# A fused attention and FFN kernel: FFN2 of batches 2 to 7 for pairs of token tiles by seven products instead of eight

## The chip, the core and the metric

The kernel runs on one core of a Trainium2 chip. The metric is the device time of one execution in microseconds (us); the number given for a kernel is the median of several runs. The core has five engines that work side by side, each through its own queue of instructions in order: TensorE (PE, matrix products; its weight loads are listed as PEld), VectorE (DVE), ScalarE (ACT), GpSimd (POOL) and SyncE (SP). Here POOL issues the loads from the main memory and SP the stores and the transposes by DMA. PE writes its sums to PSUM, eight banks of 128 x 512 numbers in f32; DVE and ACT read them from there and write to SBUF.

## The reference

```python
scores = scale * np.matmul(q, k.transpose(0, 1, 3, 2))      # 8 batches, 12 heads, 448 tokens, 64 columns; scale = 1/8
attn = np.maximum(scores, 0.0) ** 2 / S                       # S = 448
x = np.matmul(attn, v)                                        # then 3584 tokens x 768
h = x @ w_in                                                  # 768 -> 2048 (FFN1)
g = np.maximum(h, 0.0) + alpha * np.minimum(h, 0.0)
out = g @ w_out                                               # 2048 -> 768 (FFN2), in f32
```

## The kernel before

Heads are taken four at a time, so a batch has NG = 3 groups n, and there are 24 in all. A group's keys are cut into seven chunks j.

- `turn_pe` and `turn_dma` bring q and k of a group into a layout with the head's 64 columns on the partitions (tile T). From group 5 on this is `turn_dma`: DVE copies q and k into a tile `perm` (L170, two copies), and SP issues a transpose by DMA into T (L172).
- `score_mm` computes one chunk of scores: four small matmuls on PE into a pair of PSUM banks (L184). `relu` takes the pair to SBUF as `rl` on ACT ("A", L193) or DVE ("D", L195); `square` makes `at` of it, nearly always on DVE (L203).
- `attnv` multiplies the seven squared chunks of a group with v (28 matmuls, L213) into one more pair of banks; ACT empties one bank and DVE the other into xT (L223, L224).
- `f1` computes 128 of the 2048 inner columns for a batch: six matmuls (L247), then `neg` on ACT (L255) and gT on DVE (L256). A batch has 16 such units. gT holds two batches, a superblock sb, in a single buffer.
- `f2` computes one token tile of 128 for one of two column parts (256 or 512 of 768): 16 matmuls, whose fixed operand is gT and whose moving operand is w_out (L272), a copy from PSUM by ACT (L274) and two stores by SP (L280). A superblock has seven tiles; tile 3 lies half in each batch.

The kernel is written with a manual schedule: every engine's instructions stand in the order in which the program names them. PSUM banks are dealt out while the program is written, the longest unused first (`take_bank` for one, `take_pair` for a pair of neighbours); `hold` keeps a bank out of this.

From batch 2 on the order is this. The 16 f1 units of batch b come first. Chunks of the next batch's groups are computed in between: three after f1 unit 5 and three after unit 11 (`run(some(3))`), with relus on ACT, DVE, ACT. `prepare` calls `turn_dma` for a later group and sends POOL's loads of the group after next; it stands ahead of units 1 and 9 and in the FFN2 stage. Then comes the FFN2 stage with three `burst` calls between the f2 units: three chunks, the attnv of group n, two chunks, and then the squares of all five. Even batches take tiles 0 to 2 of the superblock, odd ones tiles 3 to 6. Batch 7 has no bursts.

Batches 0 and 1 have an order written out by hand. In batch 1, `turn_dma(6)` stands ahead of the f1 units' outputs, `turn_dma(7)` and `turn_dma(8)` after units 1 and 10. POOL waits for the landing of the transposes of groups 5, 6 and 8 (a copy of one element, `landed`) before it sends more loads; after group 6 these are three parts of w_out and four loads of q, k and v.

Tiles come from pools with a fixed number of buffers. A tile that takes a buffer anew waits until the last reader of the old tile has finished; for `perm` this reader is the DMA transpose.

Of the kernel before, what the change touches and what calls it, by code (L numbers as in the profile page):

```python
# [16 lines left out]
NJ = 7  # L17
# [3 lines left out]
def kernel(  # L21
# [36 lines left out]
    ident = singles.tile([128, 128], BF16)  # L58
    w_in_sb = singles.tile([128, NG, 2, d_ff], BF16)
    w_out_sb = [singles.tile([128, KF, hi - lo], BF16, name=f"w_out{i}") for i, (lo, hi) in enumerate(COLS)]  # L60
    alpha_sb = singles.tile([128, KF], F32)
# [58 lines left out]
    def load_w_out(h, lo=0, hi=KF, step=4):  # L120
        for lo in range(lo, hi, step):
            nc.gpsimd.dma_start(out=w_out_sb[h][:, lo:lo + step], in_=w_out_v[:, lo:lo + step, COLS[h][0]:COLS[h][1]])

# [12 lines left out]
    for lo, hi, eng in ((0, 4, nc.sync), (4, NJ, nc.scalar)):  # L136
        t = singles.tile([128, 2, (hi - lo) * D], F32, name=f"qfirst{lo}")
# [60 lines left out]
    def square(n, j, rl, eng="D"):  # L198
        a = at_pool.tile([128, 2, S], BF16, tag="at", name="at")
        if eng == "A":  # L200
            nc.scalar.activation(a, rl, ACTF.Square)
        else:
            nc.vector.tensor_tensor(a, rl, rl, ALU.mult)  # L203
        att[(n, j)] = a
# [38 lines left out]
    gT = {}  # L243
# [16 lines left out]
    def f1(b, ff):  # L260
        ps = take_bank()[:, :S]
        f1_mm(ps, b, ff, range(KM))
        f1_out(ps, b, ff)

    def f2(sb, c, h, parts=None):

        first_col, width = COLS[h][0], COLS[h][1] - COLS[h][0]
        o = o_pool.tile([128, d_model - CUT], F32, tag="o", name="osb")
        for lo, hi in parts or ((0, width),):
            ps = take_bank()[:, :hi - lo]  # L270
            for ff in range(KF):
                nc.tensor.matmul(ps, gT[sb][:, ff, bass.ts(c, 128)], w_out_sb[h][:, ff, lo:hi],  # L272
                                 start=(ff == 0), stop=(ff == KF - 1))
            nc.scalar.copy(o[:, lo:hi], ps)  # L274
            for u in range(2):
                blk = 2 * c + u
                b, j = 2 * sb + blk // NJ, blk % NJ
                rows = out[b * S:(b + 1) * S].rearrange("(pp j) d -> j pp d", j=NJ)
                eng = nc.scalar if u and parts else nc.sync
                eng.dma_start(out=rows[j][:, first_col + lo:first_col + hi], in_=o[64 * u:64 * u + 64, lo:hi])  # L280

# [167 lines left out]

    def some(k):  # L450
        lo = at_c[0]
        at_c[0] = min(lo + k, len(chunks))
        return [(n, j, e) for (n, j), e in zip(chunks[lo:at_c[0]], "ADA")]

    def burst(n):

        sc(some(3))
        attnv(n)
        sc(some(2))
        sq()  # L460
# [49 lines left out]
    burst(8)  # L510
    f2(0, 6, 1)

    for b in range(2, B):
# [15 lines left out]
        for i, u in enumerate(units):  # L529
            if i in at and not last:  # L530
                g = at[i]
                if g == 1:
                    prepare(n0 + 4)
                burst(n0 + g)
            if last and i == len(units) - 1:
                f2(*u, parts=((0, 384), (384, 512)))
            else:
                f2(*u)

# [29 lines left out]
```

## Time and profile before

| what | value |
|---|---|
| time, median of 3 runs | 386.65 us (385.65 to 386.66) |
| span of the profiled execution | 384.0 us |
| PE busy | 374.1 us, 97% |
| PEld busy | 205.3 us |
| DVE busy | 266.2 us, 69% |
| ACT busy | 207.6 us, 54% |
| POOL busy | 68.9 us, 18% |
| FFN1 matmuls (L247) | 768, 149.8 us |
| FFN2 matmuls (L272) | 149.8 us |
| stage of FFN2, batch 2 | 137.5 to 160.6 us |
| stage of FFN2, batch 3 | 180.4 to 208.7 us |

The profile shows one execution by its span, from the first to the last instruction; of this execution's own time beyond the span nothing is given. The runs' median is 2.65 us above the span. In the rows, the first number is busy time, and the idle time of an engine before an instruction stands with what ended it. A busy PE is not the same as a PE at its peak, since matmuls overlap in the pipeline; the chain of waits lays the pieces end to end, and its lengths per matmul are the better price.

### The profile page before, as it was taken

How to read it: one execution, taken by the hardware profiler on the slowest of the kernel's cores; microseconds unless marked ns; L12 is line 12 of the kernel's file. 1: busy time of each engine (PE TensorE's matmuls, PEld its weight loads, DVE VectorE, ACT ScalarE, POOL GpSimd, SP SyncE). 2: the span in 40 equal slices, each digit the busy share in tenths (PEclk: the TensorE clock that was granted, in tenths of full speed). 3: DMA queues.
4: the chain of work that ended last, by engine and by line, in shares of the span. 5: the costliest groups of instructions: out<-in, count | busy, mean ns of one | idle time of the engine just before them, and what ended most of it. 6: DMA issues, size and time to landing. Idle time of an engine off the chain costs nothing.

```text
span 384.0 us, 7838 instructions
## 1 busy us (share of the span) xinstructions
PE 374.1 (97%) x3171; PEld 205.3 (53%) x3192; DVE 266.2 (69%) x423; ACT 207.6 (54%) x335; POOL 68.9 (18%) x105
## 2 busy tenths in 40 slices
PE   6799999999999999999999999999999999999996
PEld 5454565555544455545565455544556445645554
DVE  3987988777657988688656887779855788526300
ACT  4988687445643754455444656546544475434321
POOL 8566050506402202022200222020000000000000
PEclk9999999999999999999999999999999999999999
DMA  9999989999995667488292772946035300120023
GB/s 145 192 204 202 186 127 199 171 178 203 224 172 109 108 113 114 105 134 119 48 167 60 134 120 53 165 76 120 15 86 88 77 1 15 43 68 2 14 68 85
DMA packets 73556, 43.29 MB, mean 113 GB/s; under 512 B 40368, under 2 KB 70064, under 8 KB 73520
## 3 DMA queue, kind: packets, MB, share of 16 engines
q0 software_dynamic: 27136, 22.58, 39.8%
q1 hardware_dynamic: 45952, 19.88, 26.8%
q8 instruction: 25, 0.41, 0.5%
q10 hardware_dynamic: 432, 0.33, 0.3%
q14 instruction: 11, 0.09, 0.1%
HBM read 45.62 MB, written 11.01 MB: 147 GB/s over the span
## 4 chain that ended last, share of the span: by engine, by line
PE 95%; DVE 2%; issue 1%; POOL 0%; ACT 0%; ACTq 0%; POOLq 0%; DVEq 0%
PE psum L247 38%; PE psum L272 38%; PE psum L184 9%; PE psum L213 8%; DVE at L203 1%; PE psum L146 1%; DVE T L165 1%; PE psum L162 1%; DVE rl L195 0%; POOL kraw L131 0%; ACT osb L274 0%; ACTq L280 0%; POOL ident masks.py:199 0%; POOL ident masks.py:197 0%; POOLq masks.py:199 0%
## 5 line engine op out<-in xcount | busy, mean ns | idle before, releaser
L272 PE MATMUL psum<-w_out,gT 128*128 128x256 bf16 (+3 forms) x891 | 149.8, 322 | 1.1
L247 PE MATMUL psum<-xT,w_in_sb 128*128 128x448 bf16 x768 | 149.8, 353 | 0.0
L272 PEld LDWEIGHTS <-gT 128*128 128x128 bf16 x912 | 86.8, 98 | 64.2 <-issue 8.2
L247 PEld LDWEIGHTS <-w_in_sb 128*128 128x128 bf16 x768 | 73.7, 98 | 72.8 <-issue 5.3
L256 DVE SCALAR_TENSOR_TENSOR gT<-neg,beta_sb,psum 128x448 bf16<-128x448 f32 x128 | 83.4, 676 | 33.8 <-ACT neg L255 33.6
L255 ACT ACTIVATE neg<-psum 128x448 f32<-128x448 f32 x128 | 69.2, 546 | 60.3 <-PE psum L247 59.2
L193 ACT ACTIVATE rl<-psum 128x896 bf16<-128x896 f32 x112 | 97.7, 930 | 1.4 <-PE psum L184 1.4
L203 DVE TENSOR_TENSOR at<-rl 128x896 bf16<-128x896 bf16 x162 | 90.5, 616 | 0.0
L195 DVE TENSOR_SCALAR rl<-psum 128x896 bf16<-128x896 f32 x56 | 60.8, 1085 | 40.4 <-PE psum L184 40.3
L274 ACT COPY osb<-psum 128x256 f32<-128x256 f32 (+3 forms) x57 | 26.9, 473 | 104.7 <-PE psum L272 97.6
L184 PE MATMUL psum<-T 64*64 64x448 bf16 x672 | 45.4, 356 | 2.1 <-DVE T L165 1.1
L100 POOL DMA_DIRECT2D qraw<-in_q_dram x23 | 16.6, 722 | 136.2 <-DVE perm L170 131.7
L213 PE MATMUL psum<-at,vraw 64*64 64x448 bf16 x672 | 36.2, 350 | 0.0
L184 PEld LDWEIGHTS <-T 64*64 64x64 bf16 x672 | 16.8, 105 | 21.0 <-issue 13.6
L213 PEld LDWEIGHTS <-vraw 64*64 64x64 bf16 x672 | 21.0, 106 | 11.7 <-issue 1.5
L224 DVE TENSOR_SCALAR xT<-psum 128x448 bf16<-128x448 f32 x24 | 15.0, 624 | 14.8 <-PE psum L213 11.0
L107 POOL DMA_DIRECT2D vraw<-in_v_dram x24 | 17.5, 732 | 4.6 <-PE psum L184 1.4
L100 POOL DMA_DIRECT2D kraw<-in_k_dram x23 | 16.7, 726 | 1.9 <-issue 1.4
L223 ACT ACTIVATE xT<-psum 128x448 bf16<-128x448 f32 x24 | 13.4, 560 | 2.3 <-PE psum L213 2.3
L170 DVE COPY perm<-qraw 128x896 bf16<-128x896 bf16 x19 | 11.6, 610 | 0.0
L170 DVE COPY perm<-kraw 128x896 bf16<-128x896 bf16 x19 | 11.6, 608 | 0.0
L117 POOL DMA_DIRECT2D w_in_sb<-in_moe_w_in_dram x16 | 10.0, 634 | 5.5 <-DMA w_in_sb<-in_moe_w_in_dram 2.3
(24 smaller groups left out, 41.6 us busy)
## 6 DMA issues: line engine op xcount, KB each, us to landing
out_dram<-osb SPq DMA_DIRECT2D x54, 128.0 KB, 2.4
vraw<-in_v_dram POOLq DMA_DIRECT2D x24, 224.0 KB, 8.5
qraw<-in_q_dram POOLq DMA_DIRECT2D x23, 224.0 KB, 4.7
kraw<-in_k_dram POOLq DMA_DIRECT2D x23, 224.0 KB, 6.9
out_dram<-osb SPq DMA_DIRECT2D x56, 64.0 KB, 2.3
w_in_sb<-in_moe_w_in_dram POOLq DMA_DIRECT2D x16, 192.0 KB, 8.1
w_out<-in_moe_w_out_dram POOLq DMA_DIRECT2D x4, 512.0 KB, 10.3
w_out<-in_moe_w_out_dram POOLq DMA_DIRECT2D x4, 256.0 KB, 8.6
```

The costliest lines, as they stand in the source:

```text
L100: nc.gpsimd.dma_start(out=t.rearrange("p m j d -> p m (j d)"), in_=flat[:, 2 * g:2 * g + 2])
L170: nc.vector.tensor_copy(p[:, i], raw.pop((n, name)).rearrange("p s j d -> p j s d"))
L184: nc.tensor.matmul(ps[64 * c:64 * c + 64, r, :S], t[64 * r:64 * r + 64, 1, j, 64 * c:64 * c + 64], t[64 * r:64 * r + 64, 0, :, 64 * c:64 * ...
L193: nc.scalar.activation(rl, ps[:, :, :S], ACTF.Relu)
L195: nc.vector.tensor_scalar(rl, ps[:, :, :S], 0.0, None, ALU.max)
L203: nc.vector.tensor_tensor(a, rl, rl, ALU.mult)
L213: nc.tensor.matmul(ps[64 * s:64 * s + 64, r, :S], vv[64 * r:64 * r + 64, s, j, :], a[64 * r:64 * r + 64, s], start=(j == 0), stop=(j == NJ ...
L247: nc.tensor.matmul(ps, w_in_sb[:, km // 2, km % 2, bass.ts(ff, 128)], xT[b][:, km // 2, km % 2, :], start=(km == 0), stop=(km == KM - 1))
L255: nc.scalar.activation(neg, ps, ACTF.Relu, scale=-1.0)
L256: nc.vector.scalar_tensor_tensor(gT[b // 2][:, ff, (b % 2) * S:(b % 2) * S + S], neg, beta_sb[:, ff:ff + 1], ps, ALU.mult, ALU.add)
L272: nc.tensor.matmul(ps, gT[sb][:, ff, bass.ts(c, 128)], w_out_sb[h][:, ff, lo:hi], start=(ff == 0), stop=(ff == KF - 1))
L274: nc.scalar.copy(o[:, lo:hi], ps)
```

## The change

Two token tiles A and B (128 tokens each) make a pair. With the 2048 inner columns cut into two halves and the 768 output columns into two halves of 384, the pair's FFN2 is a product of a 2 x 2 by a 2 x 2 block matrix. In place of eight block products (of eight matmuls of 384 columns each) there are seven, by Strassen's scheme in Winograd's form: the left operands of four products, and the right operands of four, are sums or differences of blocks.

- The sums of w_out are made once (`weight_mix`, four tiles `w_mix`, in eight halves on DVE), between the units of FFN2 of batches 0 and 1. w_out becomes a single tile.
- The sums of gT are made for every pair (`mix`, four tiles S of 128 x 1024, on DVE).
- Products are added up in PSUM where the scheme permits. Three banks serve a pair: x and y, a pair of neighbours held from `p1` to `p4`, and z. `p1` leaves a copy in SBUF (ACT); `p6` and `p7` leave sums u2 and u3 (DVE); three of the four output blocks are sums on DVE (`plus`), one is a copy on ACT. Each block is stored by two stores of SP.
- Per superblock of batches 2 to 7 there are three pairs and one tile by `f2`. In superblocks 1 and 2 the pairs are (0, 1), (3, 4), (5, 6), and tile 2 is the single one; in the last they are (0, 1), (2, 3), (4, 5), and tile 6 is the single one. Batches 0 and 1 keep `f2` for all tiles.
- The bursts from batch 2 on have other shapes: the first of a stage has three chunks (relus on ACT, ACT, DVE) ahead of the attnv and three (ACT) after it, the others two and three, all on ACT. The chunks inside f1 stages become 3 + 2 (2 + 2 for batch 2), all on ACT. Two of the bursts of a stage now stand inside or right behind a pair's products.
- Buffers: v 7 to 6, perm 3 to 1, rl 7 to 6, at 12 to 10, neg 3 to 2, o 10 to 6; new pools u (4) and S (4). The first two tiles of q use buffers of o, and some early `at` tiles use buffers of S.

```diff
-    v_pool = ctx.enter_context(tc.tile_pool(name="v", bufs=7))
-    perm_pool = ctx.enter_context(tc.tile_pool(name="perm", bufs=3))
+    v_pool = ctx.enter_context(tc.tile_pool(name="v", bufs=6))
+    perm_pool = ctx.enter_context(tc.tile_pool(name="perm", bufs=1))
...
-    rl_pool = ctx.enter_context(tc.tile_pool(name="rl", bufs=7))
-    at_pool = ctx.enter_context(tc.tile_pool(name="at", bufs=12))
+    rl_pool = ctx.enter_context(tc.tile_pool(name="rl", bufs=6))
+    at_pool = ctx.enter_context(tc.tile_pool(name="at", bufs=10))
...
-    neg_pool = ctx.enter_context(tc.tile_pool(name="neg", bufs=3))
-    o_pool = ctx.enter_context(tc.tile_pool(name="o", bufs=10))
+    neg_pool = ctx.enter_context(tc.tile_pool(name="neg", bufs=2))
+    o_pool = ctx.enter_context(tc.tile_pool(name="o", bufs=6))
+    u_pool = ctx.enter_context(tc.tile_pool(name="u", bufs=4))
+    S_pool = ctx.enter_context(tc.tile_pool(name="S", bufs=4))
...
+    def hold_pair():
+        lo = min((0, 2, 4, 6), key=lambda i: (max(taken[i], taken[i + 1]), i))
+        taken[lo] = taken[lo + 1] = 10**9
+        return lo
...
+    def weight_mix(i, lo, hi):
...
+        x, y, op = ((b12, b11, ALU.subtract), (b22, t[0], ALU.subtract),
+                    (b22, b12, ALU.subtract), (b21, t[1], ALU.subtract))[i]
+        nc.vector.tensor_tensor(t[i], x, y, op)
...
+        def mix(self, *which):
+            for i in which:
+                t = self.s[i] = S_pool.tile([128, KH, 128], BF16, tag="S", name="S")
+                x, y, op = {1: (self.a21, self.a22, ALU.add),
+                            2: (self.s.get(1), self.a11, ALU.subtract),
+                            3: (self.a11, self.a21, ALU.subtract),
+                            4: (self.a12, self.s.get(2), ALU.subtract)}[i]
+                nc.vector.tensor_tensor(t, x, y, op)
+
+        def mm(self, ps, left, right, start):
+            for i in range(KH):
+                nc.tensor.matmul(ps, left[:, i], right[:, i], start=(start and i == 0), stop=(i == KH - 1),
+                                 skip_group_check=not start)
+
+        def plus(self, ps, u, keep=None):
+            t = keep or o_pool.tile([128, d_model - CUT], F32, tag="o", name="osb")[:, :NH]
+            nc.vector.tensor_tensor(t, ps, u, ALU.add)
+            return t
...
+        def p1(self):
+            self.xy = hold_pair()
+            self.x, self.y = psum[:, self.xy, :NH], psum[:, self.xy + 1, :NH]
+            self.mm(self.x, self.a11, w_out_sb[:, :KH, :NH], True)
+            self.m1 = self.kept()
+            nc.scalar.copy(self.m1, self.x)
+
+        def p6(self):
+            self.mm(self.y, self.s[2], w_mix[1], True)
+            self.u2 = self.plus(self.y, self.m1, self.kept())
+
+        def p7(self):
+            self.mm(self.y, self.s[3], w_mix[2], False)
+            self.u3 = self.plus(self.y, self.m1, self.kept())
+
+        def p5(self):
+            self.z = take_bank()[:, :NH]
+            self.mm(self.z, self.s[1], w_mix[0], True)
+
+        def c22(self):
+            store(self.sb, self.tb, NH, d_model, self.plus(self.z, self.u3))
+
+        def p2(self):
+            self.mm(self.x, self.a12, w_out_sb[:, KH:, :NH], False)
+            t = o_pool.tile([128, d_model - CUT], F32, tag="o", name="osb")[:, :NH]
+            nc.scalar.copy(t, self.x)
+            store(self.sb, self.ta, 0, NH, t)
+
+        def p4(self):
+            self.mm(self.y, self.a22, w_mix[3], False)
+            take(self.xy, 2)
+            store(self.sb, self.tb, 0, NH, self.plus(self.y, self.m1))
+
+        def p3(self):
+            self.mm(self.z, self.s[4], w_out_sb[:, KH:, NH:], False)
+            store(self.sb, self.ta, NH, d_model, self.plus(self.z, self.u2))
+
+        def tail(self):
+            self.p7()
+            self.p5()
+            self.c22()
+            self.p2()
+            self.p4()
+            self.p3()
...
-    def burst(n):
+    def burst(n, before="ADA", after="AD"):
 
-        sc(some(3))
+        sc(some(len(before), before))
         attnv(n)
-        sc(some(2))
+        sc(some(len(after), after))
         sq()
...
     run(some(3))
+    weight_mix(0, 0, 4)
     f2(0, 5, 0)
     burst(6)
     f2(0, 2, 1)
+    weight_mix(0, 4, 8)
+    weight_mix(1, 0, 4)
     run(some(3))
     f2(0, 3, 1)
+    weight_mix(1, 4, 8)
     f2(0, 6, 0)
     prepare(10)
     burst(7)
+    weight_mix(2, 0, 4)
     f2(0, 4, 1)
+    weight_mix(2, 4, 8)
     f2(0, 5, 1)
+    weight_mix(3, 0, 4)
     burst(8)
     f2(0, 6, 1)
+    weight_mix(3, 4, 8)
...
             if not last and ff in (6, 12):
-                run(some(3))
+                run(some(2 if b == 2 or ff == 12 else 3, "AAA"))
...
         if b % 2 == 0:
-            units = [(sb, c, h) for c in range(3) for h in range(2)]
-            at = {1: 0, 3: 1, 5: 2}
+            p = Pair(sb, 0, 1)
+            p.mix(1, 2)
+            if b + 2 < B:
+                f2(sb, 2, 0)
+            p.mix(3, 4)
+            burst(n0, "AAD", "AAA")
+            prepare(n0 + 4)
+            p.p1()
+            p.p6()
+            burst(n0 + 1, "AA", "AAA")
+            if b + 2 < B:
+                p.tail()
+                burst(n0 + 2, "AA", "AAA")
+                f2(sb, 2, 1)
+            else:
+                p.p7()
+                p.p2()
+                burst(n0 + 2, "AA", "AAA")
+                p.p5()
+                p.c22()
+                p.p4()
+                p.p3()
+        elif not last:
+            p, r = Pair(sb, 3, 4), Pair(sb, 5, 6)
+            p.mix(1, 2, 3, 4)
+            burst(n0, "AAD", "AAA")
+            prepare(n0 + 4)
+            p.p1()
+            p.p6()
+            burst(n0 + 1, "AA", "AAA")
+            p.tail()
+            r.mix(1, 2, 3, 4)
+            r.p1()
+            r.p6()
+            burst(n0 + 2, "AA", "AAA")
+            r.tail()
         else:
-            units = [(sb, 3, 0), (sb, 3, 1), (sb, 4, 1), (sb, 4, 0), (sb, 5, 1), (sb, 5, 0), (sb, 6, 0), (sb, 6, 1)]
-            at = {1: 0, 4: 1, 7: 2}
...
+            p, r = Pair(sb, 2, 3), Pair(sb, 4, 5)
+            p.mix(1, 2, 3, 4)
+            p.p1()
+            p.p6()
+            p.p5()
+            p.p2()
+            p.p7()
+            p.c22()
+            f2(sb, 6, 0)
+            p.p4()
+            p.p3()
+            r.mix(1, 2, 3, 4)
+            r.p1()
+            r.p6()
+            r.p5()
+            r.p2()
+            r.p7()
+            r.c22()
+            r.p4()
+            r.p3()
+            f2(sb, 6, 1, parts=((0, 384), (384, 512)))
```

More of the change, by code (lines that the diff above doesn't have):

```diff
@@ L59 @@
     w_in_sb = singles.tile([128, NG, 2, d_ff], BF16)
-    w_out_sb = [singles.tile([128, KF, hi - lo], BF16, name=f"w_out{i}") for i, (lo, hi) in enumerate(COLS)]
+    w_out_sb = singles.tile([128, KF, d_model], BF16)
+    KH, NH = KF // 2, d_model // 2
+    w_mix = [singles.tile([128, KH, NH], BF16, name=f"w_mix{i}") for i in range(4)]
     alpha_sb = singles.tile([128, KF], F32)
@@ L121, in load_w_out @@
         for lo in range(lo, hi, step):
-            nc.gpsimd.dma_start(out=w_out_sb[h][:, lo:lo + step], in_=w_out_v[:, lo:lo + step, COLS[h][0]:COLS[h][1]])
+            nc.gpsimd.dma_start(out=w_out_sb[:, lo:lo + step, COLS[h][0]:COLS[h][1]], in_=w_out_v[:, lo:lo + step, COLS[h][0]:COLS[h][1]])
     FIRST = 4
@@ L136 @@
     for lo, hi, eng in ((0, 4, nc.sync), (4, NJ, nc.scalar)):
-        t = singles.tile([128, 2, (hi - lo) * D], F32, name=f"qfirst{lo}")
+        t = o_pool.tile([128, 2, (hi - lo) * D], F32, tag="o", name=f"qfirst{lo}")
         eng.dma_start(out=t, in_=flat0["q"][:, :, lo * D:hi * D])
@@ L198, in square @@
     def square(n, j, rl, eng="D"):
-        a = at_pool.tile([128, 2, S], BF16, tag="at", name="at")
+        if n < NG and j % 3 == 0 and j:
+            a = S_pool.tile([128, 2, S], BF16, tag="S", name="at")
+        else:
+            a = at_pool.tile([128, 2, S], BF16, tag="at", name="at")
         if eng == "A":
@@ L263, in f1, with store @@
         f1_out(ps, b, ff)
+    def store(sb, c, lo, hi, t, other=None):
+        for u in range(2):
+            blk = 2 * c + u
+            b, j = 2 * sb + blk // NJ, blk % NJ
+            rows = out[b * S:(b + 1) * S].rearrange("(pp j) d -> j pp d", j=NJ)
+            eng = other if u and other else nc.sync
+            eng.dma_start(out=rows[j][:, lo:hi], in_=t[64 * u:64 * u + 64])
     def f2(sb, c, h, parts=None):
@@ L271, in f2 @@
             for ff in range(KF):
-                nc.tensor.matmul(ps, gT[sb][:, ff, bass.ts(c, 128)], w_out_sb[h][:, ff, lo:hi],
+                nc.tensor.matmul(ps, gT[sb][:, ff, bass.ts(c, 128)], w_out_sb[:, ff, first_col + lo:first_col + hi],
                                  start=(ff == 0), stop=(ff == KF - 1))
             nc.scalar.copy(o[:, lo:hi], ps)
[L275 to L280, printed above, removed]
+            store(sb, c, first_col + lo, first_col + hi, o[:, lo:hi], nc.scalar if parts else nc.sync)
@@ new lines, in weight_mix, with __init__, kept @@
+    def weight_mix(i, lo, hi):
+        b11, b12 = w_out_sb[:, lo:hi, :NH], w_out_sb[:, lo:hi, NH:]
+        b21, b22 = w_out_sb[:, KH + lo:KH + hi, :NH], w_out_sb[:, KH + lo:KH + hi, NH:]
+        t = [w[:, lo:hi] for w in w_mix]
+        x, y, op = ((b12, b11, ALU.subtract), (b22, t[0], ALU.subtract),
+                    (b22, b12, ALU.subtract), (b21, t[1], ALU.subtract))[i]
+        nc.vector.tensor_tensor(t[i], x, y, op)
+    class Pair:
+        def __init__(self, sb, ta, tb):
+            self.sb, self.ta, self.tb = sb, ta, tb
+            ga, gb = gT[sb][:, :, bass.ts(ta, 128)], gT[sb][:, :, bass.ts(tb, 128)]
+            self.a11, self.a12, self.a21, self.a22 = ga[:, :KH], ga[:, KH:], gb[:, :KH], gb[:, KH:]
+            self.s = {}
+        def mix(self, *which):
[14 more added lines that the diff above has]
+            return t
+        def kept(self):
+            return u_pool.tile([128, NH], F32, tag="u", name="u")
+        def p1(self):
[34 more added lines that the diff above has]
+            self.p3()
@@ L448, with some @@
     at_c = [0]
-    def some(k):
+    def some(k, p="ADA"):
         lo = at_c[0]
         at_c[0] = min(lo + k, len(chunks))
-        return [(n, j, e) for (n, j), e in zip(chunks[lo:at_c[0]], "ADA")]
-    def burst(n):
-        sc(some(3))
+        return [(n, j, e) for (n, j), e in zip(chunks[lo:at_c[0]], p)]
+    def burst(n, before="ADA", after="AD"):
+        sc(some(len(before), before))
         attnv(n)
-        sc(some(2))
+        sc(some(len(after), after))
         sq()
@@ L523 @@
         if b % 2 == 0:
-            units = [(sb, c, h) for c in range(3) for h in range(2)]
-            at = {1: 0, 3: 1, 5: 2}
-        else:
-            units = [(sb, 3, 0), (sb, 3, 1), (sb, 4, 1), (sb, 4, 0), (sb, 5, 1), (sb, 5, 0), (sb, 6, 0), (sb, 6, 1)]
-            at = {1: 0, 4: 1, 7: 2}
[L529 to L538, printed above, removed]
+            p = Pair(sb, 0, 1)
[12 more added lines that the diff above has]
+                f2(sb, 2, 1)
+            else:
+                p.p7()
[19 more added lines that the diff above has]
+            r.tail()
+        else:
+            p, r = Pair(sb, 2, 3), Pair(sb, 4, 5)
[19 more added lines that the diff above has]
+            f2(sb, 6, 1, parts=((0, 384), (384, 512)))
 _INS = ['q', 'k', 'v', 'moe_w_in', 'moe_w_out', 'moe_alpha']
```

## The prediction

> **What bounds the kernel now.** I read the page's engine shares first, then the chain that ended last, then the timelines of TensorE (PE) and VectorE (DVE) over one FFN2 stage.
>
> ```profile
> PE 374.1 (97%) x3171; PEld 205.3 (53%) x3192; DVE 266.2 (69%) x423; ACT 207.6 (54%) x335; POOL 68.9 (18%) x105
> ...
> PE 95%; DVE 2%; issue 1%; POOL 0%; ACT 0%; ACTq 0%; POOLq 0%; DVEq 0%
> ```
>
> PE works 97% of the span and is 95% of the chain, so removed matmul time counts, if PE gets no waits in return. FFN2 of batch 3, PE then DVE:
>
> ```profile
> 180.38 1.91 PE L272 MATMUL psum<-w_out,gT 128*128 128x256 bf16 x16
> 182.22 0.76 PE L184 MATMUL psum<-T 64*64 64x448 bf16 x12
> 182.81 1.50 PE L213 MATMUL psum<-at,vraw 64*64 64x448 bf16 x28
> 184.13 0.55 PE L184 MATMUL psum<-T 64*64 64x448 bf16 x8
> ...
> 208.68 3.57 PE L247 MATMUL psum<-xT,w_in_sb 128*128 128x448 bf16 x18
> ```
>
> ```profile
> 182.84 1.09 DVE L195 TENSOR_SCALAR rl<-psum 128x896 bf16<-128x896 f32 x1 [1.00 <-PE psum L184]
> 184.38 0.62 DVE L224 TENSOR_SCALAR xT<-psum 128x448 bf16<-128x448 f32 x1 [0.45 <-PE psum L213]
> 184.92 1.08 DVE L195 TENSOR_SCALAR rl<-psum 128x896 bf16<-128x896 f32 x1
> 185.92 2.76 DVE L203 TENSOR_TENSOR at<-rl 128x896 bf16<-128x896 bf16 x5
> 188.59 0.61 DVE L170 COPY perm<-qraw 128x896 bf16<-128x896 bf16 x1
> 189.12 0.61 DVE L170 COPY perm<-kraw 128x896 bf16<-128x896 bf16 x1
> 194.00 1.09 DVE L195 TENSOR_SCALAR rl<-psum 128x896 bf16<-128x896 f32 x1 [4.26 <-PE psum L184]
> ```
>
> The reader is to see that PE has no gap (a burst of 5 chunks and one attnv fills 182.22 to 184.61) and that DVE waits for PE (4.26 us idle), never PE for DVE. The stage lasts 28.3 us.
>
> **What is removed.** By the chain a 256-column matmul takes 1.75/16 = 0.109 us; from ACT copy to ACT copy (361.42 to 364.87) a 512-column one takes 3.45/16 = 0.216. 384 columns lie midway: 0.1625. A product of eight is 1.30 us, seven are 9.1; two tiles cost 2 x (1.75 + 3.45) = 10.4. Saved: 1.3 us for each of nine pairs, **11.7 us**.
>
> **Prices on DVE and ACT.** DVE's bf16 copies took 225 ns for 128 elements and 613 for 896, 0.505 ns an element; the bf16 square of 896 took 616. So a mix of activations (1024) is 0.68 us, one of weights (1536) 0.94. Bounds: 0.62 (the 896 row) and 1.22 (f32 rate, 1.03 ns an element between the 448 and 896 rows from PSUM); I take the bf16 rate, since all operands are bf16. A `plus` (384, f32 from PSUM) is 0.624 - 64 x 0.00103 = 0.56, at most 0.62 by the two-operand L256 row (676 ns for 448). Consecutive DVE work starts about 0.08 earlier (five squares in 2.76: 0.535 apart), consecutive ACT relus 0.82 apart. A chunk is 0.21 us of PE, an attnv 1.32.
>
> **The waits in an FFN2 stage.** t = 0 is the stage's first PE instruction. The last gT ends at 1.46 (360.93 against 359.47 in batch 7).
> - Batches 3, 5, 6: DVE's queue now holds four mixes ahead of the burst's one DVE relu. Mix 2 needs mix 1's result: 1.5-2.2, 2.2-2.9, 2.8-3.5, 3.4-4.1; relu 4.0-5.1. The burst now has six chunks and an attnv over four PSUM pairs, so the sixth takes the third's pair, the one that this relu frees. PE would be there at 2.4 and gets it at 5.2: 2.8 lost. ACT's relus are not late.
> - Behind that relu DVE has xT (to 5.6), six squares (8.8), two perm copies (9.9, `prepare` stands before `p1`), u2 (10.35), then the next burst's xT (11.0). The second burst has three pairs, two being held; its fifth chunk reuses the attnv's pair and waits until 11.05, where PE is at 10.4: 0.65, and 0.2 on an ACT relu. p3 ends at 17.8.
> - Batches 3, 5: the second pair's mixes stand behind the first's last `plus` (18.0-18.5), so s2 is ready at 19.9; p1 fills 1.3 from 17.8, p6 waits 0.9; its burst waits 0.55. Sum 5.1; stage 18.2 + 16 x 0.21 + 3 x 1.32 + 5.1 = 30.6 against 28.3; one chunk less in the f1 stage (0.2): **+2.1 each**.
> - Batches 2, 4: a 1.75 us FFN2 unit covers part of the mixes; the sixth chunk loses 1.1, then 0.85 as above, then 0.4 (attnv on the bank that p3's `plus` frees). 21.6 + 2.35 = 24.0 against 23.1: **+0.5 and +0.7** with two and one chunks (0.2 each) gone from the f1 stage.
> - Batch 6: 15.4 + 3.65 = 19.1 against 22.0 (a tile went to batch 7), a chunk less: **-3.1**.
> - Batch 7: p6 waits for s2 (3.0 against 1.3): 1.7; the second pair's p6 0.9; its p4 follows p7 at once on the same bank and waits for u3: 0.85. 18.2 + 1.75 + 3.45 = 23.4 up to the last unit, against 17.4: **+6.0**.
> Together **+8.3**: 22 us of waits less about 2 that these stages had, against 11.7 saved. Bounds for the waits: mixes at 0.62 take off about 1.5, at 1.22 they add about 13; I keep +4 to +13, since neighbouring waits overlap.
>
> **Weight mixes.** Eight of 0.94 on DVE between 91 and 119 us, 7 us where DVE idled about 12. Two stand ahead of a burst's DVE relu and delay it by up to 0.9 and 1.7, of which chunk and FFN2 work covers half: **+1.0** (0 to 3).
>
> **perm from three buffers to one.** Each perm copy on DVE now waits until the transpose before has landed. Later transposes are 9.7 us or more apart and land in 6 to 7.6, so they are free. In batch 1 the copies come 2.4 and 7.7 us apart. SP's queue and landings, us from issue (rows of T6, T8, T10, T11, T13 in turn):
>
> ```profile
> 62.48 1.55 SPq L172 DMA_TRANSPOSE T<-perm  x1
> T<-perm SPq DMA_TRANSPOSE x1, 4.8
> ...
> 72.64 5.76 SPq L172 DMA_TRANSPOSE T<-perm  x1
> T<-perm SPq DMA_TRANSPOSE x1, 14.6
> ...
> 104.10 5.93 SPq L172 DMA_TRANSPOSE T<-perm  x1
> T<-perm SPq DMA_TRANSPOSE x1, 11.6
> ...
> 121.48 1.55 SPq L172 DMA_TRANSPOSE T<-perm  x1
> T<-perm SPq DMA_TRANSPOSE x1, 6.2
> ...
> 148.78 3.54 SPq L172 DMA_TRANSPOSE T<-perm  x1
> T<-perm SPq DMA_TRANSPOSE x1, 7.6
> ```
>
> T6 lands at 67.3; T7's copy moves from 63.7 to there, its transpose from 64.9 to 68.5. Behind the copy nine gT are queued: PE's eleventh f1 unit, which needs the third's bank, waits 0.8. T8's copy (71.4 before) waits for T7, and five gT wait behind it, which FFN2's first unit, ending at 77.6 before, needs. It ends 4.3 us (copies 1.07, five gT 3.0, rest) after T7 lands. POOL sends w_out and others (2.4 MB) from 67.85, beside T7. T11 and T13 met fresh loads so; T8 and T10 met a queue filled before. I take 7.6 (T13): 76.1 + 4.3 - 77.6 = **+2.8**; ends +0.8 (landed by 73) and +9.8 (14.6).
> The Trainium skill ("DMA: Bandwidth & Descriptors", Queues, rings and completion order) has each engine go round its queues packet by packet, which would hold T7 near T11's 6.2 us, +1.4; T8's 14.6 speaks against leaning on it.
>
> A pair's eight stores on SP carry the bytes that the two tiles' eight carried, so SP's queue stays as it is. The fewer rl, at, v, neg and o buffers I cost at nothing: stores land in 2.4 us and a buffer comes round after several units; if that cover is gone, an ACT copy waits 2 to 3 us with PE's bank behind it. ACT gets relus at 0.82 where it is busy 54%. The end's drain is unchanged.
>
> **Sum.** The profiled execution's span is 384.0; 8.3 + 1.0 + 2.8 = 12.1 makes 396.1. The median of the runs lies 2.65 above the span: 386.65 + 12.1 = **398.8 us**.
>
> **Rivals.**
> - T7 lands as late as T10 or T8 (11.6, 14.6): 402.8 to 405.8. For it: 2.4 MB go out at the same time; against: T7's issue meets an empty queue.
> - PE runs slower after its waits. For it: after the idle start 28 matmuls of 128 columns took 3.17 us, 113 ns each, against 1.10/16 = 69 for 128 columns at the end; against: the granted clock is 1.00 in all later stretches, though no gap tests it. If each of seven places gave 28 such matmuls' extra 1.2 us: 407. The skill's "TensorE: Matmul & The Clock Gate" (Part 1) halves the clock after an idle window of some 3.4 us; by it only the batch 1 wait could reach that, and would cost about 1.7 us, an estimate.
> - Faster: DVE reaches the burst's relu in time because the mixes are short. With mixes at nothing about 17 of the 22 us of waits go: 382. It decides at mixes of about 0.2 us, where 12 go. Against it: no 896-element DVE row is under 0.60.
>
> **Chances.** Forecast case 0.58, late T7 0.22, slower PE 0.10, short mixes 0.10 (0.08 faster, 0.02 within 0.3%, about what a measurement here can tell from no change). Slower 0.90. The range leaves out the faster case and about a tenth above: 390 to 407: the low bounds (386.65 + 4 + 0 + 0.8 = 391.5) a little widened, and the late T7 with about 1 us more.
>
> **What would show it.** Right: PE busy share falls below 93%; PE's score matmuls wait 2 us at a time for a DVE relu at the start of FFN2 stages; DVE's perm copies wait for a transpose near 68 and 75; batch 3's stage near 30.6 us, product matmuls 0.16 us. Wrong: mixes well off 0.68 us, or PE's chain still unbroken over an FFN2 stage, which ends near 377.

## The result, and the profile after

The changed kernel takes **411.34 us** (410.46 to 412.2) against 386.61 for the kernel before: 1.065 times as long, 95% interval 1.063 to 1.067. The direction was forecast, the size was not: 24.7 us instead of 12.1, and above the range. The profiled execution was the slowest of the four (412.2 us); its span of 410.3 us is 26.3 more than that of before, where other runs with a span of 384.0 took 385.8, below their median. So the two traces differ by 1.6 us more than the medians.

Line numbers below are those of the kernel the line comes from. The page of the changed kernel: engine shares, shares of the chain that ended last, and the clock granted to PE, one digit for each fortieth of the span.

```profile
PE 376.7 (92%) x3120; PEld 201.7 (49%) x3120; DVE 291.5 (71%) x480; ACT 225.1 (55%) x349; POOL 68.9 (17%) x105
...
PEclk9999999959999999999999999999999998999999
...
PE 74%; DVE 12%; DMA 6%; ACT 5%; issue 2%; POOL 0%; ACTq 0%; DVEq 0%; POOLq 0%
```

72 matmuls are gone (the page of before lists 3171 of its 3192), yet PE is busy 2.6 us longer than before, and a quarter of the chain belongs to other engines. The clock digits say where to look first: a 5 in the ninth slice (82 to 92 us), and an 8 late in the run. PE's three largest waits, summed by what it waits for (us in total, times, longest):

```profile
PE psum L292 <- DVE gT L268: 10.1, 5, 8.9
PE psum L193 <- DVE rl L204: 7.3, 6, 1.8
PE psum L326 <- DVE S L322: 3.5, 4, 1.5
```

The first is one place in batch 1. The second is the first burst of the FFN2 stages: 1.77 us in batches 3, 5 and 6, 0.73 and 0.84 in 2 and 4, and 0.42 in batch 1. The third is the operand of a pair's second product. PE in that place in batch 1 (start, us):

```profile
76.63 1.36 PE L292 MATMUL psum<-w_out_sb,gT 128*128 128x256 bf16 x11
86.94 0.40 PE L292 MATMUL psum<-w_out_sb,gT 128*128 128x256 bf16 x1 [8.95 <-DVE gT L268]
...
91.23 3.16 PE L292 MATMUL psum<-w_out_sb,gT 128*128 128x256 bf16 x16
```

The chain of waits of the same stretch, and the landing time of group 7's transpose (T7):

```profile
61.38 7.87 PE psum L259 x42
69.25 15.78 DMA T<-perm
...
85.15 1.15 DVE perm L179 x2
86.30 0.60 DVE gT L268
```

```profile
T<-perm SPq DMA_TRANSPOSE x1, 15.8
```

T7 is issued at 69.25 and lands 15.8 us later. Until then DVE stands before `turn_dma(8)`'s copy, with five gT behind it, and PE, which needs them, idles 8.95 us. The windows over it: start and end, length, busy time of PE, PEld, DVE, ACT and POOL (instructions), granted clock, DMA share, GB/s.

```profile
80.00:85.00 5.00, 0.00 (x0) 0.00 (x0) 0.00 (x0) 0.00 (x0) 0.00 (x0) 0.52 1.24 196
85.00:90.00 5.00, 1.93 (x9) 0.55 (x11) 4.28 (x7) 1.63 (x3) 0.00 (x0) 0.50 0.97 170
90.00:95.00 5.00, 5.00 (x41) 2.72 (x40) 2.75 (x5) 2.67 (x5) 3.93 (x7) 0.62 0.67 100
```

The clock has fallen to a half by the time the gT come, so the next unit of 16 matmuls (91.23) takes 3.1 us instead of 1.75. FFN2 of batch 3 on PE, then on DVE, at the places shown of before:

```profile
195.81 0.76 PE L193 MATMUL psum<-T 64*64 64x448 bf16 x12
...
197.23 1.51 PE L225 MATMUL psum<-at,vraw 64*64 64x448 bf16 x26 [0.47 <-DVE gT L268]
198.39 0.72 PE L193 MATMUL psum<-T 64*64 64x448 bf16 x8
200.88 0.38 PE L193 MATMUL psum<-T 64*64 64x448 bf16 x4 [1.77 <-DVE rl L204]
201.20 1.47 PE L326 MATMUL psum<-w_out_sb,gT 128*128 128x384 bf16 x8
202.51 1.46 PE L326 MATMUL psum<-w_mix,S 128*128 128x384 bf16 x8
...
215.63 1.47 PE L326 MATMUL psum<-w_mix,S 128*128 128x384 bf16 x8 [0.68 <-DVE S L322]
```

```profile
197.21 0.69 DVE L322 TENSOR_TENSOR S<-gT 128x1024 bf16<-128x1024 bf16 x1
...
199.14 0.68 DVE L322 TENSOR_TENSOR S<-gT,S 128x1024 bf16<-128x1024 bf16 x1
199.74 1.08 DVE L204 TENSOR_SCALAR rl<-psum 128x896 bf16<-128x896 f32 x1
```

This is the forecast picture: four mixes of 0.68 us, the burst's DVE relu behind them, and the sixth chunk on PE at 200.88 behind that. The stage lasts 30.76 us (195.81 to 226.57), before 28.3.

All 26.3 us, by the lag of PE's landmarks in the two traces (the same first or last matmul of a stage):

| place | forecast, us | measured, us |
|---|---|---|
| up to the first f1 unit of batch 1 (60.60, after 61.31) | 0 | +0.7 |
| from there to the end of the first FFN2 unit of batch 1 (77.58, 89.97) | +2.8 | +11.7 |
| the next FFN2 unit, to 80.82 and 95.02 | 0 | +1.8 |
| rest of batch 1, with the weight mixes (117.77, 132.58) | +1.0 | +0.6 |
| batch 2, 3, 4, 5 | +0.5, +2.1, +0.7, +2.1 | +0.7, +2.4, +1.3, +2.4 |
| batch 6 | -3.1 | -1.3 |
| batch 7 up to the last unit (376.85, 403.06) | +6.0 | +5.9 |
| sum | +12.1 | +26.2 |

The first row is not the change: in the executions of the kernels below this matmul starts between 60.33 us (changed up to there) and 61.49, and at 61.26 in one that is the kernel before up to there. Of batch 6's 1.8 too much, 1.7 are the clock, 0.66 on average between 345 and 350 us: two products take 4.39 us from the first's start to the next matmul, where the same two in batch 5 take 2.70.

```profile
346.20 2.59 PE L326 MATMUL psum<-w_out_sb,gT 128*128 128x384 bf16 x8
348.59 2.07 PE L326 MATMUL psum<-w_mix,S 128*128 128x384 bf16 x8
350.59 0.57 PE L193 MATMUL psum<-T 64*64 64x448 bf16 x8
```

### The profile page after: what moved, and what is told of

It reads as the page before. It is cut to its first block, busy times and chain, and to the rows that moved or that the text cites. A ratio compares the mean times of both kernels' runs of the same rounds, so it can differ in the third digit from the quotient of the medians.

```text
span 410.3 us, 7828 instructions
## 1 busy us (share of the span) xinstructions
PE 376.7 (92%) x3120; PEld 201.7 (49%) x3120; DVE 291.5 (71%) x480; ACT 225.1 (55%) x349; POOL 68.9 (17%) x105
## 4 chain that ended last, share of the span: by engine, by line
PE 74%; DVE 12%; DMA 6%; ACT 5%; issue 2%; POOL 0%; ACTq 0%; DVEq 0%; POOLq 0%
PE psum L259 31%; PE psum L326 20%; PE psum L292 11%; PE psum L193 6%; DMA T<-perm 6%; DVE S L322 4%; PE psum L225 4%; ACT rl L202 2%; DVE gT L268 2%; DVE rl L204 2%; ACT neg L267 1%; ACT xT L235 1%; DVE perm L179 1%; DVE at L215 1%; PE psum L171 1%
## 5 line engine op out<-in xcount | busy, mean ns | idle before, releaser
L202 ACT ACTIVATE rl<-psum 128x896 bf16<-128x896 f32 x144 | 124.2, 933 | 19.1 <-PE psum L193 19.1
L268 DVE SCALAR_TENSOR_TENSOR gT<-neg,beta_sb,psum 128x448 bf16<-128x448 f32 x128 | 84.9, 678 | 32.2 <-ACT neg L267 30.6
L292 PE MATMUL psum<-w_out_sb,gT 128*128 128x256 bf16 (+3 forms) x336 | 57.6, 325 | 10.3 <-DVE gT L268 10.1
L193 PE MATMUL psum<-T 64*64 64x448 bf16 x672 | 51.5, 365 | 10.7 <-DVE rl L204 7.3
L292 PEld LDWEIGHTS <-gT 128*128 128x128 bf16 x336 | 32.3, 100 | 35.5 <-DVE gT L268 11.9
L326 PE MATMUL psum<-w_mix,S 128*128 128x384 bf16 x216 | 38.9, 330 | 3.5 <-DVE S L322 3.5
L326 PEld LDWEIGHTS <-S 128*128 128x128 bf16 x288 | 27.5, 99 | 24.5 <-DVE S L322 5.1
L204 DVE TENSOR_SCALAR rl<-psum 128x896 bf16<-128x896 f32 x24 | 26.1, 1086 | 9.6 <-PE psum L193 8.3
L294 ACT COPY osb<-psum 128x256 f32<-128x256 f32 (+3 forms) x21 | 9.7, 462 | 39.9 <-PE psum L292 37.3
L331 DVE TENSOR_TENSOR osb<-psum,u 128x384 f32<-128x384 f32 x27 | 15.1, 558 | 21.6 <-PE psum L326 20.2
L326 PEld LDWEIGHTS <-gT 128*128 128x128 bf16 x216 | 21.0, 99 | 15.6 <-issue 2.7
L326 PE MATMUL psum<-w_out_sb,gT 128*128 128x384 bf16 x144 | 27.5, 336 | 0.0
L236 DVE TENSOR_SCALAR xT<-psum 128x448 bf16<-128x448 f32 x24 | 14.9, 620 | 11.7 <-PE psum L225 10.5
```

Source lines behind the costliest of these rows:

```text
L193: nc.tensor.matmul(ps[64 * c:64 * c + 64, r, :S], t[64 * r:64 * r + 64, 1, j, 64 * c:64 * c + 64], t[64 * r:64 * r + 64, 0, :, 64 * c:64 * ...
L202: nc.scalar.activation(rl, ps[:, :, :S], ACTF.Relu)
L204: nc.vector.tensor_scalar(rl, ps[:, :, :S], 0.0, None, ALU.max)
L268: nc.vector.scalar_tensor_tensor(gT[b // 2][:, ff, (b % 2) * S:(b % 2) * S + S], neg, beta_sb[:, ff:ff + 1], ps, ALU.mult, ALU.add)
L326: nc.tensor.matmul(ps, left[:, i], right[:, i], start=(start and i == 0), stop=(i == KH - 1), skip_group_check=not start)
```

## The experiments

Theory 1: the extra loss is the single `perm` buffer, through T7's late landing and the clock behind it. Its rivals: the FFN2 stages lose more than forecast; or the loss in batch 1 has another cause.

**The wait removed.** The copies for groups 7 and 8 go to two weight-mix tiles that nobody uses yet; `perm` keeps one buffer otherwise.

```diff
-        p = perm_pool.tile([128, 2, NJ, 2, D], BF16, tag="perm", name="perm")
+        if n in (7, 8):
+            flat = w_mix[n - 5].rearrange("p k c -> p (k c)")[:, :4 * NJ * D]
+            p = flat.rearrange("p (a j s d) -> p a j s d", a=2, j=NJ, s=2)
+        else:
+            p = perm_pool.tile([128, 2, NJ, 2, D], BF16, tag="perm", name="perm")
```

> The changed kernel, with the copies of groups 7 and 8 written to two w_mix tiles that are still unused then, so that neither waits for the transpose before it. Theory 1 (the single perm buffer is the cause of the batch 1 wait): VectorE's waits for a transpose near 64 and 75 us are gone, FFN2's first unit ends near 78.3 us instead of 90.0, its second takes 1.75 us instead of 3.09, and the time falls by 13 to 14 us, to 397 to 398.5. Rival (the loads starve the transposes whatever waits for them, and their late landing then holds up the scores or the next copy): the time falls by less than 7 us, with a new wait for T on TensorE or for a transpose at the copy of group 9.

Measured: 398.78 us (397.77 to 399.99), 1.033 times before (1.030 to 1.036), 12.6 below the changed kernel; 13 to 14 were expected, and under 7 by the rival. The first FFN2 unit of batch 1 ends at 77.32 instead of 89.97, and the clock is 1.00 throughout 75 to 95 us. So the buffer in batch 1, with what follows from it, is half of the loss.

**The wait alone, in the kernel before.**

```diff
-    perm_pool = ctx.enter_context(tc.tile_pool(name="perm", bufs=3))
+    perm_pool = ctx.enter_context(tc.tile_pool(name="perm", bufs=1))
```

> The kernel before with one perm buffer and nothing else changed. Theory 1: it loses 12 to 15 us (399 to 402), all of it between 63 and 95 us, and TensorE's granted clock falls to about a half there. Rival (the other buffers, the single w_out tile or the new order are needed for the wait): it loses under 3 us.

Measured: 398.69 us (397.59 to 399.32), 1.032 times before (1.029 to 1.035). This one line costs 12.2 us, within the 12 to 15 that were expected. The copy of group 8 on DVE, and the chain ahead of it, in this kernel:

```profile
83.94 0.62 DVE L170 COPY perm<-qraw 128x896 bf16<-128x896 bf16 x1 [10.74 <-DMA T<-perm]
```

```profile
67.94 15.88 DMA T<-perm
```

The two experiments agree from both sides, so the term does not depend on the pairs. It is half of the 24.7; the other half stands in the FFN2 stages of the table. Left to ask are why T7 is so late, what the clock adds, and what the stages wait for.

**Loads sent only after T7.** The changed kernel; POOL sends its 2.4 MB (w_out, q, k, v) when T7 has landed, not T6.

```diff
-            nc.gpsimd.tensor_copy(landed, T[6][:1, 0, 0, :1])
-            load_w_out(1, 4)
-            load_qk(9)
-            load_v(6)
-            load_v(7)
...
+        if ff == 1:
+            nc.gpsimd.tensor_copy(landed, T[7][:1, 0, 0, :1])
+            load_w_out(1, 4)
+            load_qk(9)
+            load_v(6)
+            load_v(7)
```

> The changed kernel, one perm buffer, but GpSimd sends w_out and the other loads of batch 1 only once the transpose of group 7 has landed. Theory 2 (the 15.8 us landing comes from those loads): group 7 lands 4 to 6 us after its issue, VectorE's wait of 10 us falls to 0 to 1; w_out comes some 5 us later and FFN2's first 512-column unit may wait for it 0 to 4 us; time 398 to 403. Rival (a transpose is as slow by itself when it starts from a single buffer): the landing stays above 10 us and the time stays within 3 us of 411.

Measured: 403.89 us (402.49 to 404.52), 1.045 times before, 0.9 above the expected range. The landings of T6, T7 and T8 here, us from issue (stretches 60 to 64, 66 to 72, 73 to 80):

```profile
T<-perm SPq DMA_TRANSPOSE x1, 4.0
...
T<-perm SPq DMA_TRANSPOSE x1, 4.2
...
T<-perm SPq DMA_TRANSPOSE x1, 16.0
```

Without the loads T7 lands in 4.2 us; now T8, issued beside them, takes 16.0, and the copy of group 9 waits for it:

```profile
91.66 0.62 DVE L179 COPY perm<-qraw 128x896 bf16<-128x896 bf16 x1 [6.72 <-DMA T<-perm]
```

So it is the loads: a transpose that is issued beside these 2.4 MB lands after about 16 us, one with none beside it after about 4. The wait moved by one group, and 7.5 of the 12.6 us came back.

**PE kept busy in the wait.** 135 spare matmuls of 128 columns into an unused bank, before the matmul that waits.

```diff
+                if (sb, c, h, ff) == (0, 3, 0, 11):
+                    spare = psum[:, min(range(8), key=lambda i: (taken[i], i)), :128]
+                    for _ in range(135):
+                        nc.tensor.matmul(spare, ident, ident, start=True, stop=True)
```

> The changed kernel with 135 spare matmuls of 128 columns (about 7.6 us of work whose result nobody reads) placed where TensorE waits 9 us in batch 1. Theory 3 (TensorE's clock falls because it idles there): the granted clock stays 1.00 from 80 to 95 us, the next unit takes 1.75 us instead of 3.09, time about 2 us less (409 to 410), although work was added. Rival (the clock has another cause, or the long unit has): the unit stays near 3 us, the time does not fall or grows by up to 1 us.

Measured: 410.73 us (410.55 to 410.9), 0.6 below the changed kernel's median and within the spread of its runs, not 2: a miss. The windows show why, columns as above:

```profile
80.00:85.00 5.00, 5.00 (x93) 5.00 (x91) 0.62 (x2) 0.00 (x0) 0.00 (x0) 1.00 1.25 196
85.00:90.00 5.00, 2.62 (x24) 1.04 (x21) 3.66 (x7) 2.16 (x5) 0.18 (x1) 0.89 0.89 149
90.00:95.00 5.00, 5.00 (x42) 2.74 (x35) 3.89 (x6) 3.28 (x5) 4.49 (x7) 0.77 0.85 126
```

The spare work holds the clock at 1.00 during the wait. Then the last five matmuls come one at a time, after 0.81 us of idleness and with 0.3 to 0.5 us between them as each gT is made, and the clock falls after all: the next unit takes 2.7 us instead of 3.1, not 1.75. That the clock falls with PE's idleness is shown, and also that it does not take one long wait: short ones, 2.4 us of 3.9, did it as well.

**The FFN2 stages: the relu taken off DVE's queue.** From here on the base is the first experiment's kernel (398.78). In even and odd batches, the first burst's last relu ahead of the attnv moves to ACT.

```diff
-            burst(n0, "AAD", "AAA")
+            burst(n0, "AAA", "AAA")
```

> e1 (398.8 us) with the one VectorE relu of a stage's first burst on ScalarE; the four mixes stay where they are. Theory 4 (TensorE waits for that relu's bank, and this is the loss): the sixth chunk's wait of 2 us in batches 3, 5, 6 and 1 us in 2, 4 goes and the stages end that much earlier, 8 to 10 us less, 389 to 391. Theory 5 (VectorE's whole queue from the mixes to the second burst's xT is the limit, and the relu's bank is only the first place where it shows): the wait moves to the second burst's fifth chunk, which waits for xT; only the relu's own 1.0 us per stage is won, 4 to 6 us less, 393 to 395.

Measured: 392.42 us (391.91 to 392.65), 1.015 times before (1.014 to 1.017): 6.4 less, between the two theories' ranges. PE's waits for `rl` of DVE fall from 7.3 us to 0.4 us; its waits for ACT's relus rise from 1.4 to 2.1, and 1.2 appear for xT:

```profile
PE psum L197 <- ACT rl L206: 2.1, 7, 0.4
PE psum L197 <- DVE xT L240: 1.2, 2, 0.6
PE psum L197 <- DVE rl L208: 0.4, 1, 0.4
```

So 5.0 us of waits are gone. Part of the 6.4 is the clock: the base's profiled execution lost 1.7 us by it in batch 5, this one nothing, and the base's four runs have mean clocks of 0.987 to 0.996, these 0.994 to 1.000.

**The sums of gT left out.** Each product takes a block of gT itself, so the four sums of a pair are not computed.

```diff
-                t = self.s[i] = S_pool.tile([128, KH, 128], BF16, tag="S", name="S")
-                x, y, op = {1: (self.a21, self.a22, ALU.add),
...
-                nc.vector.tensor_tensor(t, x, y, op)
+                self.s[i] = {1: self.a21, 2: self.a11, 3: self.a11, 4: self.a12}[i]
```

> e1 with the sums of gT left out: the products take blocks of gT itself in their place (so this part of the computation is changed), all else as it was. Theory 6 (the mixes on VectorE are the larger part of what FFN2's stages wait for): batch 3's stage falls from 30.8 to about 27.4 us, batch 7's by 2.6, the whole by 13 to 16 us, to 383 to 386. Rival (the held banks, the sums after the products and ScalarE's relus hold TensorE anyway): less than 8 us is won, over 391.

Measured: 384.52 us (383.52 to 384.7), 0.995 of before (0.993 to 0.996). The sums cost 14.3 us: with them gone the kernel is 2.0 us faster than before. Between the two traces PE's waits fall by 11.5 us and its busy time by 2.1, of which 1.7 are the base's clock drop. Both experiments say the same of the stages: the loss is what PE waits for in DVE's queue, not the products.

**The same work in another order.** All sums kept; two `perm` buffers (paid for with one buffer each of o and u). The first burst's DVE relu is the first of its chunks and stands ahead of the mixes; mixes 3 and 4 come behind the second attnv; p5 comes ahead of p7; the next pair's mixes 1 and 2 come ahead of p4, 3 and 4 behind p3; the `perm` copies (`prepare`) move behind the first pair's products. In batch 7, tile 6's first unit comes behind p1. Its core, for odd batches:

```diff
-            p.mix(1, 2, 3, 4)
-            burst(n0, "AAD", "AAA")
-            prepare(n0 + 4)
+            sc(some(3, "DAA"))
+            p.mix(1, 2)
+            attnv(n0)
+            sc(some(3, "AAA"))
+            sq()
             p.p1()
             p.p6()
-            burst(n0 + 1, "AA", "AAA")
-            p.tail()
-            r.mix(1, 2, 3, 4)
+            sc(some(2, "AA"))
+            attnv(n0 + 1)
+            sc(some(3, "AAA"))
+            p.mix(3, 4)
...
+            r.mix(1, 2)
+            p.p4()
+            p.p3()
+            r.mix(3, 4)
+            prepare(n0 + 4)
```

> e1 with the same work in another order, and two perm buffers (o 5, u 3): the VectorE relu is the first of its burst; two mixes stand behind the first three chunks and two behind the second burst's xT; the copies for the transpose come late in the stage; the second pair's first two mixes stand ahead of the last sums of the first pair; a product stands between p7 and p4; batch 7 puts FFN2 of tile 6 behind p1. Theory 5 and 6 (only the order of VectorE's queue is at fault; its work fits): stages of 22.8, 27.3, 22.8, 27.3, 17.2 us and batch 7 some 3.4 us shorter, 15 to 18 us less than e1, 381 to 384, faster than before (386.5). Rival (VectorE has too much work in these stages in any order): waits come back in other places, no faster than 388.

Measured: 386.67 us (385.82 to 386.85), 1.000 of before (0.999 to 1.001). 12.1 us come back without one sum less, but the forecast of 381 to 384 is missed: batch 3 takes 28.8 us, and what is left at PE in it are ACT's relus in the bursts (0.43, 0.19, 0.43) and the first attnv's bank (0.47). The first of these:

```profile
190.72 2.76 PE L330 MATMUL psum<-w_mix,S 128*128 128x384 bf16 x16 [0.43 <-ACT rl L206]
```

**Chunks set between the products.** The bursts are taken apart: behind p1 an attnv and two chunks, behind p6 two chunks, an attnv and two more, behind p2 two; no relu on DVE. Its core, for the first pair of odd batches, against the last kernel:

```diff
+            p.mix(1, 2)
-            sc(some(3, "DAA"))
-            p.mix(1, 2)
+            sc(some(3, "AAA"))
+            p.p1()
+            sq(2)
             attnv(n0)
-            sc(some(3, "AAA"))
-            sq()
-            p.p1()
+            sc(some(2, "AA"))
+            sq(3)
             p.p6()
             sc(some(2, "AA"))
+            sq(1)
             attnv(n0 + 1)
-            sc(some(3, "AAA"))
             p.mix(3, 4)
+            sc(some(2, "AA"))
+            p.p2()
+            sc(some(2, "AA"))
             sq(3)
-            p.p5()
             p.p7()
             sq()
-            p.p2()
+            p.p5()
```

> All seven products are kept, with two staging buffers for the reshaping, as in the reordered kernel, which came out at 386.67 us, level with the kernel before. What is left there by its trace: the product that follows a burst of four groups of score matmuls starts with all of ScalarE's relus behind it, and the first attention product of a stage waits 0.95 us for a bank. Here the groups are set between the products instead of in one burst: the first product of a stage comes ahead of the first attention product, two groups follow the product after it, and the fifth product comes behind the seventh, so that no relu has more than about two groups to keep up with. If what the reordered kernel still loses is the engines' pace within bursts, batches 3 and 5 take 26.0 to 26.5 us instead of 28.8, batches 2 and 4 about 22.2 instead of 23.7, batch 6 about 16.1 instead of 17.2, batch 7 stays at 19.95, and the time is 377 to 381 us, faster than before. If the loss is the sums that each product waits for (VectorE's own total of sums and copies), spreading the groups moves the waits to other matmuls, and the time stays at 385 us or above.

Measured: **381.31 us** (380.94 to 382.08) against 385.88, **0.988 of before (0.987 to 0.990)**: 1.2% faster, 0.3 us above the range that was expected. Batches 3 and 5 take 27.0 us, 2 and 4 23.1, batch 6 16.5, batch 7 19.95. All but batch 7 are 0.4 to 1 us longer than expected, though the trace shows no wait of PE in these stages. (The wait of 0.95 us for a bank that the expectation names is 0.47 in the reordered kernel's trace.) The shares and a stretch of batch 3 in this kernel:

```profile
PE 369.0 (97%) x3120; PEld 196.3 (52%) x3120; DVE 286.2 (76%) x475; ACT 227.2 (60%) x354; POOL 68.9 (18%) x105
```

```profile
184.78 1.47 PE L330 MATMUL psum<-w_mix,S 128*128 128x384 bf16 x8
186.18 0.57 PE L197 MATMUL psum<-T 64*64 64x448 bf16 x8
...
193.23 1.46 PE L330 MATMUL psum<-w_mix,gT 128*128 128x384 bf16 x8
194.53 1.46 PE L330 MATMUL psum<-w_out_sb,S 128*128 128x384 bf16 x8
```

From start to start, the product before a chunk takes 1.40 us, products in a row 1.30. The span is 5.2 us shorter than before, where 11.7 us of matmuls are gone. The trace of before changes between 64 x 64 and 128 x 128 matmuls 50 times after 118 us, this one 82 times.

**The price of a change of form, alone.** The kernel before, with the chunks inside FFN1 stages computed one at a time between units instead of three together: 40 changes more, nothing else.

```diff
-            if not last and ff in (6, 12):
-                run(some(3))
+            if not last and ff in (6, 7, 8, 12, 13, 14):
+                run([(n, j, "ADA"[ff % 6 % 3]) for n, j, e in some(1)])
```

> The kernel before, with one edit: the two groups of three score chunks in each FFN1 stage of batches 2 to 6 are computed one chunk at a time, ahead of units 6, 7, 8 and 12, 13, 14. The same instructions run; PE changes between the 64 x 64 matmuls of the scores and the 128 x 128 matmuls of FFN1 twelve times in a stage instead of four, 40 more changes in all. In the interleaved kernel a product that stands alone between score matmuls took 1.40 us where products in a row are 1.30 apart, and two chunks between products 0.48 to 0.51 where they take 0.41 between their like. If each change of the form costs PE those 0.07 to 0.1 us whatever stands around it, this kernel is 2.8 to 4 us slower than before. If the 0.1 belongs to the products (their sums, their banks), the time is within 0.5 us of before.

Measured: 391.09 us (390.21 to 391.47) against 386.62, 1.012 times before (1.010 to 1.013): 4.5 us, 3.8 to 5.1, for 40 changes, so 0.11 us each, a little above the 0.07 to 0.1 that were expected. In its trace a chunk and the unit behind it take 1.55 us:

```profile
169.11 0.38 PE L184 MATMUL psum<-T 64*64 64x448 bf16 x4
169.42 1.31 PE L247 MATMUL psum<-xT,w_in_sb 128*128 128x448 bf16 x6
170.66 0.38 PE L184 MATMUL psum<-T 64*64 64x448 bf16 x4
```

Alone they would be 0.21 and 1.14. PE's table of waits gains only one DMA wait of 0.4 us at the start: the rest counts as busy time (380.0 us against 374.1). The Trainium skill ("TensorEngine Tiling (Array Packing)", Key Properties) states that changing the tiling mode drains TensorE, without a figure; the run agrees, and gives one. Of the 11.7 us that the interleaved kernel saves in matmuls, its 32 extra changes would take 3.5 by that price, an estimate; 5.2 are left in the span, and the other 3 were not followed. Nor was it run whether eight products with chunks between them would gain; the kernel before has no wait of PE in these stages to win back.

## Why the prediction failed, step by step

- **The step that failed: T7's landing.** The prediction took 7.6 us, T13's row, with 14.6 as the far end; it was 15.8 in the changed kernel and 15.9 in the kernel before with one buffer. It chose by the issue ("T7's issue meets an empty queue"). But the prediction itself had T7 go out at 68.5 and POOL's loads from 67.85 (69.25 and 68.49 in the trace), so the loads' queue was being filled ahead of it. T13 stood beside three loads (0.67 MB), T7 beside seven (2.4 MB), and it landed about when they did: at 85.03, with the fourth and fifth at 84.3 and 85.6. The nearest row was T8's, 14.6 behind the same loads. The rest of that term's working held: "it ends 4.3 us after T7 lands" was 85.03 to 89.97, 4.9, and with 15.8 it gives +11.0 for the measured +11.7. The rival "late T7" was the right case; it was given 0.22, and its 405.8 was still 5.5 too low, since T7 came later yet and the clock stood at nothing.
- **The round robin of queues.** From the Trainium skill ("DMA: Bandwidth & Descriptors", Queues, rings and completion order) the prediction estimated 6.2 us for T7, and did not lean on it. Landings of 15.5 to 16.0 us in four kernels beside the loads, and of 4.0 to 4.8 ahead of them, speak against that estimate. Why the transposes wait so long was not tried.
- **"Later transposes are free."** They landed in up to 10.4 us, not 7.6. In batch 4 one took 10.41 us from 230.28, the next copy waited 1.66, and the stage lasted 24.6 where batch 2's lasted 24.2. About 0.4 us.
- **The clock was costed at nothing.** The rival "PE runs slower after its waits" was half right. In batch 1 the estimate by the Trainium skill ("TensorE: Matmul & The Clock Gate", Part 1) was 1.7 us, and the row is 1.8: the trace agrees. But batch 6 lost another 1.7 at waits of at most 1.77 us, half of that page's idle window, which by the prediction could not happen. The first experiment's execution lost the same 1.7 in batch 5 instead, and had batch 6 at 19.1, as forecast; the third's had drops in both. The same page says that the activity window runs free (What's actually happening), and that many short idle times can throttle PE too (A second HAM failure mode). The traces agree, and show which stage is hit. From 20 us on, the clock of the changed kernel's execution changes between 1.00 and 0.50 at 80.16, 93.81, 346.40 and 349.81 us: 4, 74 and 1 steps of 3.41 us. In the third experiment's it does so at 286.61, 290.02, 337.81 and 341.22: 1, 14 and 1 steps. PE's busy time within the step that contains the 1.77 us wait decides:

| kernel, stage | step, us | PE busy in it, us | clock in the next step |
|---|---|---|---|
| changed, batch 6 | 342.98 to 346.40 | 1.65 | 0.50 |
| changed, batch 5 | 291.78 to 295.20 | 1.89 | 1.00 |
| first experiment, batch 5 | 278.61 to 282.02 | 1.65 | 0.50 |
| first experiment, batch 6 | 329.81 to 333.22 | 1.68 | 1.00 |
| third experiment, batch 3 | 187.62 to 191.04 | 1.66 | 1.00 |
| third experiment, batches 5, 6 | 283.20 to 286.61, 334.40 to 337.81 | 1.64, 1.65 | 0.50 |

In these executions and the fourth experiment's, a step at full clock with PE busy 1.65 us or less (0.48 of it) was followed by one at half clock, which costs 1.7 us; none with 1.66 or more was. The ends of matmuls are modelled, so the border is known only as about a half. Where the steps lie against a wait differs between executions: which of these stages lost 1.7 us is luck.
- **The FFN2 stages were right.** Batches 2, 3, 5 and 7 came within 0.3 us of the forecast, the sixth chunk in batch 3 at 5.07 us of the stage where 5.2 was worked out, p6 of the second pair 0.68 late where 0.9 was. Not foreseen: the first attnv's 0.47 us for the last gT's bank. Mixes measured 0.68, weight mixes 0.95, `plus` 0.56, a product 1.30, all as priced within 0.01. "With mixes at nothing about 17 of the 22 us of waits go": 11.5 went, and 14.3 of time.
- **Weight mixes**: +0.6 for +1.0. The other buffers gave PE no wait that the traces show.
- **What would show it**: PE's share (92%, forecast below 93), the 2 us waits for the DVE relu (1.8), the waits for `perm` (3.53 ahead of the copy at 68.04, 9.97 ahead of the one at 85.15, forecast near 75) and the stage of 30.6 (30.76) all came.

Of the 14.1 us between the forecast and the table's sum, 8.9 are T7's landing, 3.5 the clock, 0.7 the start and 1.0 all else. The mechanisms were named; the sum failed on the row chosen for one landing, and on the clock that follows a wait. Nor is it shown that the scheme itself does not pay: of the 24.7 us lost, 12.6 were one buffer, and with the sums in another order and chunks between products the same seven products are 1.2% faster than eight.

## What to carry to other kernels

When a pool's last reader is a DMA, taking a buffer away turns that DMA's landing time into a wait on the engine that writes the tile: price it with the slowest landing seen beside the same loads, and count what is queued behind the writer. Less matmul work pays only if the sums it needs stand in the vector engine's queue behind whatever PE wants sooner; look at the queue's order before its load. Keep the matrix engine busy for more than about half of every 3.4 us, or the clock adds its own loss to a wait: here 1.7 us each time. And cutting bursts finer to hide such work costs about 0.1 us for every change between matmul tile forms, which the profile books as busy time.

## What the runs showed of the hardware that was not expected

- A DMA transpose that lands after about 4 us with no loads beside it takes 15.5, 15.8, 15.9 and 16.0 us when 2.4 MB of loads on another queue go out beside it, and 13.4 to 14.6 when it is issued about 5 us after the first of them.
- PE's granted clock changes only on a grid of 3.41 us whose place differs between executions. After a step in which PE was busy 1.65 us or less it was 0.50 for the next, after 1.66 or more it stayed at 1.00: so one wait of 1.77 us, with one of 0.47 beside it, cost 1.7 us more in one stage and nothing in others of the same shape. Once at a half it stayed there after a step with PE busy 2.29 us and rose after one with 3.41.
- Single matmuls with 0.3 to 0.5 us between them, after 0.8 us of idleness, let the clock fall from 1.00 to 0.50 (0.77 on average over the next 5 us) after PE had been fully busy for 8 us.
- A change between 64 x 64 and 128 x 128 matmuls costs 0.11 us (0.10 to 0.13).
